# Gated linear attention and a mixture of experts on one core: the second chunk's experts by halves of the batch, transposes of its second half by DMA, and the decay's DMA on another queue

## The chip, the core and the metric

The kernel runs on one core of a Trainium2 chip. The metric is the device time of one execution in microseconds, the median over several executions.

A core has five engines that run side by side, each with its own queue of instructions, taken in order: PE (TensorE, matrix multiply into the banks of PSUM), ACT (ScalarE), DVE (VectorE), POOL (GpSimd) and SP (SyncE, which here only issues DMAs). ACT and POOL can issue DMAs too, and an engine does so in its own order of instructions.

## The reference

The first part is an attention with a gated state. Per batch and head it keeps a 48 x 48 state; each step of the sequence decays it by a sigmoid gate, adds an outer product of k and v, and reads it with q. The second part sends each of the 3072 tokens through four experts and sums their outputs by weights.

```python
# q, k, v, f_logit: (4, 8, 768, 48)
f = 1.0 / (1.0 + np.exp(-f_logit))
for t in range(S):
    state = f[:, :, t, :, None] * state + einsum('bhd,bhe->bhde', k[:, :, t], v[:, :, t])
    y[:, :, t] = einsum('bhd,bhde->bhe', q[:, :, t], state)
x = y.transpose(0, 2, 1, 3).reshape(3072, 384)
p = domain_probs / (domain_probs.sum(-1, keepdims=True) + 1e-09)
for e in range(4):
    h = np.maximum(x @ w1[e], 0.0)          # w1[e]: 384 x 1024
    out += p[:, e:e + 1] * (h @ w2[e])      # w2[e]: 1024 x 384
```

## The kernel before

**Chunks.** The sequence of 768 steps is cut into six chunks of 128 (`c` from 0 to 5), and each chunk is worked on for all four batches (`b`), eight heads at a time in four pairs. A chunk so gives 4 x 128 = 512 tokens. For each chunk the attention makes `xT`, the 512 tokens transposed to 384 features in three tiles of 128 partitions, and then the four experts (`e`) run on `xT`. The experts of one chunk and the attention of the next are interleaved.

**Attention of one chunk and batch.** ACT makes the gates (`gate1`, `gate2`, L256 and L260) from the loaded `f`. PE sums their logarithms along time with a triangular matrix (`pe_cs`, L264). ACT makes two tiles of exponentials of these sums (`exps`): `e[:, 0]` with the sign turned (L272 for the first chunk, L274 for the others) and `e[:, 1]` (L276). POOL or DVE multiplies q by the first and k by the second (`product`, L288). Q and K so made, tile `qk`, are needed with the features on the partitions, tile `QK`: in the first two chunks PE transposes them (`pe_tp`, L297, eight transposes a batch into PSUM) and ACT or DVE copies them out; in the others a DMA transposes them (`dma_tp`, L301, SP's queue). PE then multiplies K by Q (`pe_at`, L312), DVE masks the product (L316), and PE makes y from it, from v in bf16 (`vb`, L222 or L224) and from the state `sb` (`pe_y`, L323 and L327). y is copied out as `yb` and transposed to `xT`, in the first two chunks by PE (`pe_xt`, L352, three transposes a batch and a copy), in the others by DMA (`dma_xt`, L305).

**State.** PE multiplies k and v (`pe_kv`, L333), DVE adds that to the state `Sf` (L340), and POOL multiplies the sum by the chunk's total decay `egs` (L347) and casts it to `sb` (L348). The total decay is the last row of `e[:, 0]`, 192 numbers, which have to lie on partitions instead of along a row. In the first chunk it is made by small matmuls and an activation (L278). In the others two DMAs from SP's queue move it out of the tile of exponentials (`dma_egs`, L283).

**Experts.** A unit `h` is three matmuls into one PSUM bank (`mm_h`, L356), for 128 of the 1024 hidden features and either all 512 tokens or half of them (256). ACT (L364) or DVE (L362) evicts it with a relu to the tile `h`. A unit `o` is four matmuls of 384 columns (`mm_o`, L368); two units accumulate in one bank for one batch's 128 tokens, and ACT (L377) or DVE (L375, L379) scales the bank by the token's weight and adds it to `o`, which SP stores (L383). Four PSUM banks (`ps_m`) serve `h` and `o`; four more (`ps_t`) serve the attention, and two buffers hold the tile `h` of an expert. In the first chunk expert 0, and in the second chunk experts 0 and 1, run on half the tokens at a time: first on those of batches 0 and 1 (`LO`), then on those of batches 2 and 3 (`HI`), so that they can begin before the attention of the last batches is done. All other experts run on all 512.

**What sets the order.** Nothing in the program is scheduled by the compiler. Each step is an `Op` with a priority, the steps it needs, the buffers that it takes and frees, and an assumed cost on each engine that could do it. `Plan.run` goes through them in order of assumed time, gives each free engine the ready step of the best priority, and so fixes which engine does it and the order of each engine's queue. The steps are then emitted in that order, and semaphores keep them correct whatever their real durations are. `zip_units(hs, os)` gives `h` and `o` units alternating priorities, `unit[0]` counts them, and `attention(c, slot, gran)` puts the steps of a chunk's attention at slots counted from a unit (`base`).

**The head.** Before the first expert can run, its weights have to land. POOL issues their DMAs (L235) after the last q load of the first chunk has landed, and SP issues the loads (L228) one by one. Between the first attention steps PE runs matmuls on a constant tile (`busy`, L598) that nobody reads; the plan puts as many as fit in PE's planned idle time before the first expert:

```python
for o in done:
    if o.engine == "PE" and o.start <= first:
        o.pad, t = int((o.start - t) / 0.4), o.end
```

## Time and profile before

| | us |
|---|---|
| median of 11 runs | 304.79 (303.82 to 306.3) |
| the profiled execution, its own time | 304.19 |
| its span, first to last instruction | 302.5 |
| PE busy in the span | 291.7 |
| ACT, DVE, POOL busy | 170.4, 133.4, 98.3 |

The expert matmuls are most of it: L356 152.9 us in 648 matmuls (144 of them with 256 columns, 504 with 512) and L368 151.5 us in 776; spans of matmuls that follow each other overlap, so their sums are a little above the time they hold PE. In a line of a time line the first number is the start in us from the span's start, the second the length, then engine, line, operation, tiles, shape and count; brackets give the engine's idle time before it and what ended it. In a line of the waits stand the waiting line, what it waited for, the sum in us, the number of times and the longest.

### The profile page before, as it was taken

To read this page: it belongs to the slowest core of one execution; us is meant where nothing else is said; L and a number is where in the kernel's file an instruction comes from. 1 tells how busy PE (TensorE), PEld (TensorE's weight loads), DVE (VectorE), ACT (ScalarE), POOL (GpSimd) and SP (SyncE) were. 2 spreads that over 40 slices of the span, in tenths; PEclk is the share of its full clock that TensorE was granted. 3 is DMA by queue.
4 is the path that set the end of the run, shared out by engine and by line. 5 is a ranking of instruction groups with operands and counts; after the bars stand their busy time and mean duration, and the time that the engine had idled before them with its cause. 6 is when DMAs were issued, how large, how long until landed. Compare 5 with 4: busy or idle time off the path is not lost.

```text
span 302.5 us, 5499 instructions
## 1 busy us (share of the span) xinstructions
PE 291.7 (96%) x2120; PEld 167.9 (56%) x2120; DVE 133.4 (44%) x254; ACT 170.4 (56%) x305; POOL 98.3 (33%) x161
## 2 busy tenths in 40 slices
PE   6869999999999999999999999999999999999995
PEld 3548555556876566455555556555555555555553
DVE  6576003587755486506374425353315252201223
ACT  4765673757678363677455586435575444475440
POOL 4476501325666147342533442522342100000000
PEclk9598999999999999999999999999999999999999
DMA  9999999993999689989799978200322201100002
GB/s 151 194 188 203 208 208 201 187 138 108 149 188 134 95 132 171 242 118 173 122 193 164 201 157 154 48 15 24 104 61 49 51 13 42 70 8 2 0 0 104
DMA packets 135055, 36.08 MB, mean 119 GB/s; under 512 B 125405, under 2 KB 134237, under 8 KB 135029
## 3 DMA queue, kind: packets, MB, share of 16 engines
q1 hardware_dynamic: 128416, 29.40, 56.2%
q0 software_dynamic: 6576, 6.29, 12.8%
q8 instruction: 16, 0.26, 0.4%
q14 instruction: 11, 0.08, 0.1%
q10 hardware_dynamic: 36, 0.05, 0.1%
HBM read 31.51 MB, written 4.72 MB: 120 GB/s over the span
## 4 chain that ended last, share of the span: by engine, by line
PE 89%; DMA 4%; SPq 3%; DVE 1%; issue 1%; ACT 0%
PE ps_m L356 41%; PE ps_m L368 41%; SPq L228 3%; DMA w_sb<-in_moe_w_dram 2%; PE ps_t L312 2%; DMA q<-in_q_dram 2%; PE ps_t L327 1%; DVE qk L288 1%; PE ps_t L323 1%; PE ps_t L333 1%; PE ps_t L264 1%; PE ps_t L297 1%; PE ps_t L352 0%; ACT e L274 0%; DVE o L375 0%
## 5 line engine op out<-in xcount | busy, mean ns | idle before, releaser
L356 PE MATMUL ps_m<-xT,w_sb 128*128 128x512 bf16 (+1 forms) x648 | 152.9, 357 | 0.7 <-DMA w_sb<-in_moe_w_dram 0.7
L364 ACT ACTIVATE h<-ps_m 128x512 bf16<-128x512 f32 (+1 forms) x173 | 96.8, 562 | 100.7 <-PE ps_m L356 93.5
L368 PE MATMUL ps_m<-w_sb,h 128*128 128x384 bf16 (+1 forms) x776 | 151.5, 324 | 0.0
L368 PEld LDWEIGHTS <-h 128*128 128x128 bf16 x776 | 74.0, 98 | 58.3
L375 DVE SCALAR_TENSOR_TENSOR o<-ps_m,pn,o 128x384 f32<-128x384 f32 (+1 forms) x73 | 44.5, 611 | 105.8 <-PE ps_m L368 101.9
L356 PEld LDWEIGHTS <-w_sb 128*128 128x128 bf16 x648 | 62.2, 98 | 46.4 <-DMA w_sb<-in_moe_w_dram 0.8
L288 POOL TENSOR_TENSOR qk<-q,e 128x384 bf16<-128x384 f32 x19 | 22.7, 1195 | 47.7 <-ACT e L274 41.8
L362 DVE TENSOR_SCALAR h<-ps_m 128x512 bf16<-128x512 f32 (+1 forms) x43 | 23.7, 565 | 26.7 <-PE ps_m L356 23.8
L316 DVE TENSOR_TENSOR AT<-ps_t,mask 128x512 bf16<-128x512 f32 x48 | 30.2, 684 | 10.2 <-PE ps_t L312 10.2
L347 POOL TENSOR_TENSOR Sf<-Sf,egs 48x192 f32<-48x192 f32 x40 | 20.4, 509 | 41.0 <-DVE Sf L340 39.0
L288 POOL TENSOR_TENSOR qk<-k,e 128x384 bf16<-128x384 f32 x20 | 21.3, 1065 | 15.8 <-ACT e L276 10.5
L274 ACT ACTIVATE e<-ps_t 128x384 f32<-128x384 f32 x20 | 17.3, 865 | 3.9 <-POOL sb L348 2.1
L340 DVE TENSOR_TENSOR Sf<-Sf,ps_t 48x192 f32<-48x192 f32 x40 | 14.0, 350 | 6.2 <-PE ps_t L333 5.2
L235 POOL DMA_DIRECT2D w_sb<-in_moe_w_dram x11 | 9.0, 822 | 19.5 <-DMA k<-in_k_dram 16.3
L377 ACT ACTIVATE o<-ps_m,pn 128x384 f32<-128x384 f32 x22 | 12.8, 580 | 3.2 <-PE ps_m L368 2.3
L348 POOL CAST sb<-Sf 48x192 bf16<-48x192 f32 x40 | 13.6, 339 | 2.6
L224 POOL CAST vb<-v 128x384 bf16<-128x384 f32 x19 | 10.1, 554 | 9.4 <-DMA v<-in_v_dram 3.8
L256 ACT ACTIVATE ex<-f 128x768 f32<-128x768 f32 (+1 forms) x14 | 10.5, 747 | 4.2 <-DMA f<-in_f_logit_dram 4.2
L276 ACT ACTIVATE e<-ps_t 128x384 f32<-128x384 f32 x24 | 12.7, 530 | 0.0
L327 PE MATMUL ps_t<-vb,AT 128*128 128x48 bf16 x192 | 11.6, 186 | 0.2 <-ACT vb L222 0.2
L327 PEld LDWEIGHTS <-AT 128*128 128x128 bf16 x192 | 10.1, 98 | 2.3 <-issue 0.3
L260 ACT ACTIVATE gp<-ex 128x768 bf16<-128x768 f32 (+1 forms) x14 | 10.5, 749 | 0.3
(53 smaller groups left out, 130.3 us busy)
## 6 DMA issues: line engine op xcount, KB each, us to landing
out_dram<-o SPq DMA_DIRECT2D x23, 192.0 KB, 1.9
w_sb<-in_moe_w_dram POOLq DMA_DIRECT2D x5, 768.0 KB, 18.3
k<-in_k_dram SPq DMA_DIRECT2D x10, 384.0 KB, 5.8
q<-in_q_dram SPq DMA_DIRECT2D x10, 384.0 KB, 6.1
v<-in_v_dram SPq DMA_DIRECT2D x10, 384.0 KB, 5.4
f<-in_f_logit_dram SPq DMA_DIRECT2D x9, 384.0 KB, 4.8
w_sb<-in_moe_w_dram POOLq DMA_DIRECT2D x6, 384.0 KB, 9.0
f<-in_f_logit_dram SPq DMA_DIRECT2D x6, 192.0 KB, 4.5
```

The source lines that it names most:

```text
L274: nc.scalar.activation(out=e[:, 0].rearrange("t (d h) -> t h d", d=D), in_=cs[:, 0:HD].rearrange("t (i r d) -> t r i d", r=2, d=D), func=A ...
L288: engines[eng].tensor_tensor(out=tl("qk", c, b)[:, j, :, 0:D].rearrange("t (i r) d -> t i r d", r=2), in0=tl("qk"[j], c, b // 2)[:, hh(b), ...
L316: nc.vector.tensor_tensor(out=tl("AT", c, b)[:, r].rearrange("s i t -> s (i t)"), in0=tl("A", c, b, r).rearrange("s i t -> s (i t)"), in1= ...
L327: nc.tensor.matmul(out=y[:, h * D:(h + 1) * D], lhsT=AT[:, r, i, :], rhs=vb[:, h, :], start=(c == 0), stop=True, skip_group_check=True)
L340: nc.vector.tensor_tensor(out=Sf[rows, b], in0=Sf[rows, b], in1=KV[rows, :, r, :], op=ALU.add)
L347: nc.gpsimd.tensor_tensor(out=Sf[rows, b], in0=Sf[rows, b], in1=eg, op=ALU.mult)
L348: nc.gpsimd.tensor_copy(out=nb[rows, b, :, r * D:(r + 1) * D], in_=Sf[rows, b])
L356: nc.tensor.matmul(out=tl("hp", c, e, fc, n0)[:, n0:n1], lhsT=w1_sb[:, e, kk, fc * 128:(fc + 1) * 128], rhs=tl("xT", c)[:, kk, n0:n1], sta ...
L362: nc.vector.tensor_relu(out=dst, in_=src)
L364: nc.scalar.activation(out=dst, in_=src, func=AF.Relu)
L368: nc.tensor.matmul(out=tl("op", c, e, nt, part)[:, cols], lhsT=tl("h", c, e)[:, fc, nt * T:(nt + 1) * T], rhs=w2_sb[:, e, fc, cols], start ...
L375: nc.vector.scalar_tensor_tensor(out=o, in0=op, scalar=pe, in1=o, op0=ALU.mult, op1=ALU.add)
```

## The change

1. In the second chunk (`c == 1`) all four experts run first on the tokens of batches 0 and 1, then all four on those of batches 2 and 3, each expert in halves of 256 tokens. The tile `h` of such a half is a buffer of its own (`half_of`), still two buffers in all.
2. In the second chunk, batches 2 and 3 have Q, K and x transposed by DMA (as all later chunks do) and their K times Q products run as one group; batches 0 and 1 keep PE's transposes.
3. The total decay is moved by one DMA a batch, issued by ACT right behind the exponentials, in place of two issued by SP. For that the first tile of exponentials is laid out with 64 places a head of which 48 are used, the unused ones set to zero once at the start by POOL, so that the 128 partitions of `egs` are the row as it stands.
4. The slots of the attention move: of the third chunk by 10 units to the front, of later chunks by 6. The loads of the third chunk come 8 units later.
5. The number of matmuls on the constant tile in the head is made from other assumed lengths, and a load of the first chunk is assumed a little longer.

```diff
@@
+    for i in range(rooms["e"]):
+        pads["e", i] = const.tile([T, 2 * NP * P2 + HD], FP32, name=f"e{i}")
+        nc.gpsimd.memset(pads["e", i][:, 0:2 * NP * P2].rearrange("t (r d i) -> t r d i", r=2, i=NP)[:, :, D:P2, :], 0.0)
@@
+    def e_part(c, b, j):
+
+        e = tl("e", c, b)
+        if j == 0 and c > 0:
+            return e[:, 0:2 * NP * P2].rearrange("t (r d i) -> t i r d", r=2, i=NP)[:, :, :, 0:D]
+        e = e[:, 2 * NP * P2:] if j else e[:, 0:HD]
+        return e.rearrange("t (i r d) -> t i r d", d=D, r=2)
+
     def exps(c, b):
-        cs, e = tl("cs", c, b), tl("e", c, b)
+        cs = tl("cs", c, b)
+        src = cs[:, 0:HD].rearrange("t (i r d) -> t i r d", r=2, d=D)
+        for j in range(2):
+            o, i = e_part(c, b, j), src
+            if j == 0 and c > 0:
+                o, i = (x.rearrange("t i r d -> t r i d") for x in (o, i))
+            nc.scalar.activation(out=o, in_=i, func=AF.Exp, scale=1.0 if j else -1.0)
...
-        else:
-            nc.scalar.activation(out=e[:, 0].rearrange("t (d h) -> t h d", d=D),
-                                 in_=cs[:, 0:HD].rearrange("t (i r d) -> t r i d", r=2, d=D), func=AF.Exp, scale=-1.0)
-        nc.scalar.activation(out=e[:, 1], in_=cs[:, 0:HD], func=AF.Exp)
...
     def dma_egs(c, b):
-        last = tl("e", c, b)[T - 1:T, 0].rearrange("o (d r i) -> o r d i", r=2, d=D)
-        for r in range(2):
-            nc.sync.dma_start(out=tl("egs", c, b)[r * P2:r * P2 + D, :], in_=last[:, r])
+        nc.scalar.dma_start(out=tl("egs", c, b), in_=tl("e", c, b)[T - 1:T, 0:2 * NP * P2].rearrange("o (m i) -> o m i", i=NP))
@@
+    def half_of(c, n0):
+        return n0 // N2 if c == 1 else 0
+
     def relu(c, e, fc, n0, n1, eng):
-        dst, src = tl("h", c, e)[:, fc, n0:n1], tl("hp", c, e, fc, n0)[:, n0:n1]
+        dst, src = tl("h", c, e, half_of(c, n0))[:, fc, n0:n1], tl("hp", c, e, fc, n0)[:, n0:n1]
@@
-        op = P.add(f"ld {nm}{c}.{b}", {"DMA": cost or 1.05 * n}, lambda e: load(c, nm, b, n), prio,
+        op = P.add(f"ld {nm}{c}.{b}", {"DMA": cost or (1.05 if c else 1.1) * n}, lambda e: load(c, nm, b, n), prio,
@@
-            GS.append(P.add(f"egs {c}.{b}", {"DMA": 1.0}, on(dma_egs), s(3), deps=[ex], takes=[("egs", c, b)],
-                            frees=[("e", c, b)], lag=2.0) if c and more else None)
+            GS.append(P.add(f"egs {c}.{b}", {"ACT": 0.07}, on(dma_egs), s(0) + 0.15, deps=[ex], takes=[("egs", c, b)],
+                            frees=[("e", c, b)], lag=2.8) if c and more else None)
@@
-            if c < 2:
+            if (c, b) < (1, 2):
                 tq = P.add(f"tpq {c}.{b}", {"PE": 0.22}, on(pe_tp, 0), s(4), deps=[qm],
@@
-        pairs = [[b] for b in range(B)] if c < 2 else [[b, b + 1] for b in range(0, B, 2)]
+        pairs = [[b] for b in range(B)] if c == 0 else ([[0], [1]] if c == 1 else [[0, 1]]) + [[2, 3]]
@@
-            if c < 2:
+            if (c, b) < (1, 2):
                 xdone[c, b] = []
@@
     for c in range(C):
         u0 = unit[0]
+        if c + 1 < C:
+            base = u0 + {0: 10, 1: -10}.get(c, -6)
+            attention(c + 1, lambda b, s, base=base: base + 2 + 5 * b + s, 2)
+        if c + 2 < C:
+            for half in range(2):
+                for j, nm in enumerate("fkqv"):
+                    add_load(c + 2, nm, 2 * half, 2, u0 + {0: 38}.get(c, 30) + 4 * half + j, deps=wd[3, 1])
...
         elif c == 1:
             zip_units([], ol(0, E - 1, ALL))
-            for n0, n1, xs in ((0, N2, LO), (N2, NT, HI)):
-                zip_units(hl(c, 0, n0, n1, xs), [])
-                zip_units(hl(c, 1, n0, n1, xs), ol(c, 0, xs))
+            zip_units(hl(c, 0, 0, N2, LO), [])
+            for e in range(1, E):
+                zip_units(hl(c, e, 0, N2, LO), ol(c, e - 1, LO))
+            zip_units(hl(c, 0, N2, NT, HI), ol(c, E - 1, LO))
+            for e in range(1, E):
+                zip_units(hl(c, e, N2, NT, HI), ol(c, e - 1, HI))
+            zip_units(hl(c + 1, 0, 0, NT, ALL), ol(c, E - 1, HI))
+        elif c == 2:
+            pass
         else:
             zip_units(hl(c, 0, 0, NT, ALL), ol(c - 1, E - 1, ALL))
-        for e in range(2 if c == 1 else 1, E):
+        for e in range(E if c == 1 else 1, E):
             zip_units(hl(c, e, 0, NT, ALL), ol(c, e - 1, ALL))
-        if c + 1 < C:
-            base = u0 + (0 if c else 10)
-            attention(c + 1, lambda b, s, base=base: base + 2 + 5 * b + s, 2)
-        if c + 2 < C:
-            for half in range(2):
-                for j, nm in enumerate("fkqv"):
-                    add_load(c + 2, nm, 2 * half, 2, u0 + 30 + 4 * half + j, deps=wd[3, 1])
@@
-            o.pad, t = int((o.start - t) / 0.4), o.end
+            o.pad, t = int((o.start - t) / (0.42 if t < 7.0 else 0.25)), o.end
```

## The prediction

> **What bounds the kernel now.** I read the page first: engine shares, the 40 slices, the chain of work that ended last.
>
> ```profile
> PE 291.7 (96%) x2120; PEld 167.9 (56%) x2120; DVE 133.4 (44%) x254; ACT 170.4 (56%) x305; POOL 98.3 (33%) x161
> PE   6869999999999999999999999999999999999995
> PEclk9598999999999999999999999999999999999999
> ...
> PE 89%; DMA 4%; SPq 3%; DVE 1%; issue 1%; ACT 0%
> ```
>
> TensorE carries the run. From the fourth slice on its row is all nines, so a gain has to come from fewer PE instructions, from a PE wait, or from the head, where PE is not full and its clock row shows 5 and 8. Second came the waits of PE alone, which name all it waited for:
>
> ```profile
> PE ps_t L264 <- ACT gp L260: 1.9, 2, 1.1
> PE ps_m L598 <- DVE busy L143: 1.5, 1, 1.5
> PE ps_t L297 <- DVE qk L288: 1.4, 4, 0.5
> PE ps_t L352 <- ACT yb L222: 1.4, 1, 1.4
> PE ps_m L356 <- DMA w_sb<-in_moe_w_dram: 0.7, 1, 0.7
> ```
>
> All but the L297 row lie in the head. The time line of PE places three waits of that row at the second chunk, and the head's wait for weights at 22.92:
>
> ```profile
> 59.76 0.62 PE L297 MATMUL ps_t<-ident,qk 128*128 128x128 bf16 x8 [0.43 <-DVE qk L288]
> 61.34 0.62 PE L297 MATMUL ps_t<-ident,qk 128*128 128x128 bf16 x8 [0.31 <-DVE qk L288]
> 72.93 0.40 PE L297 MATMUL ps_t<-ident,qk 128*128 128x128 bf16 x4 [0.20 <-DVE qk L288]
> ...
> 22.92 1.46 PE L356 MATMUL ps_m<-xT,w_sb 128*128 128x256 bf16 x6 [0.67 <-DMA w_sb<-in_moe_w_dram]
> ```
>
> These 0.94 us are the only ones that an edit to the middle can win; after 73 us the sums by stretch show PE busy without a break. Third, I cut the head into stretches at the steps of the clock (start:end, length, busy time, instructions, granted clock, DMA share, GB/s):
>
> ```profile
> 4.54:7.95 3.41, 2.25 (x17) 1.00 1.32 191
> 7.95:11.37 3.42, 2.94 (x22) 0.50 1.27 194
> 11.37:14.78 3.41, 3.41 (x32) 0.50 1.34 197
> 14.78:18.19 3.41, 2.82 (x44) 1.00 1.41 189
> 18.19:21.61 3.42, 1.70 (x31) 1.00 1.26 182
> 21.61:25.02 3.41, 2.74 (x22) 0.50 1.23 203
> ```
>
> A stretch with 66% or 50% busy is followed by half clock, one with 83% is not. The drop at 21.61 falls on the first expert matmuls: nine of 256 columns take 2.10 us from 22.92 on the chain of waits, where six at full clock take 0.66 on that chain, so nine take about 1.0.
>
> [...] The trace does not decide if ACT and SP block each other: the one DMA on ACT's queue took 0.63 us beside SP's first loads. [...] the L288 product on DVE takes 1.34 us at 71.55 beside POOL's and 0.64 at 74.63 beside none.
>
> **The change part by part**, the order of each engine's instructions taken from the two programs.
>
> *PE work.* The third and fourth batch of the second chunk lose 16 transposes of Q and K and 6 of x. In the stream, eight L297 take 0.45 us (75.79 to 76.24) and three L352 0.17: 0.90 and 0.34 us less. Their QK products now come in one group of 16 (0.55 us at 103.27 before) in place of two of 8 (0.33 each): 0.11 less. All four experts of that chunk now run in halves: 48 matmuls of 512 columns become 96 of 256. On the chain three of 512 take 0.65 us and six of 256 take 0.66: the trace shows nothing to 0.01 per three, so at most 0.16 for 16 such groups; I take 0.12. Sum: 1.23 us less, on the path, since PE is full.
>
> *The PE wait at 72 to 75 us.* The 0.20 at 72.93 goes with its transposes. What comes next is worse. Nine units of 256 columns (27 matmuls, three a unit, 0.325 us a unit) now follow each other from 71.59, with nothing between them, on four PSUM banks. The fourth takes the bank of the last L368 group of the chunk before. Its reader L375 stands on DVE behind the first k product, which waits for ACT (71.51) and takes 1.33 beside POOL; so that reader starts at 72.80, as it did before, and ends at 73.40. The fourth unit would start at 71.59 + 3 x 0.325 = 72.57: a wait of 0.9. The relus then start on ACT at 73.0 (next part) and clear a bank each 0.37 us, DVE joins at about 74.5: no more than 0.1. Net +0.75 with the lost 0.20 (bounds 0.2 and 1.6).
>
> *Total decay from ACT's queue.* 32 issues leave SP, 16 come to ACT, most early ones in pairs behind four exponentials.
>
> ```profile
> L283 SPq DMA_DIRECT2D egs<-e x32: 507/582/2163, 63.3 to 187.9; - x32
> ```
>
> SP gains 32 x 0.58 = 18.6 us that no PE wait needed. On ACT, the first of a pair issues beside the exponentials; the second needs the third exponential and runs 0.58 beside the fourth (0.53), so relus behind it start some 0.45 us later. Four banks cover that except at 72.6, counted above: nothing more. If an issue also waits for SP's loads it is another matter (rival 2). Landing is 2 us, and the state on POOL needs it 8 us later.
>
> *Layout of the exponentials.* The L274 write has a stride of four floats in place of eight. It took 865 ns against L276's 530; it may fall to 530 or stay. I take 865; a gain would only shorten ACT, which is 56% busy. The three memsets on POOL (0.20 each by the row of U's memset) move the mask from 3.4 to about 4.1 us; its first reader runs at 11.36: nothing.
>
> *DMA transposes.* Two of Q and K land in 3.3 us, issued at about 74.1 and 75.4: 78.7, and PE wants them at 79.4 + 0.9. Two of x land some 10 us before their half is wanted, after four experts on the first half (about 21 us). Loads stand behind them on SP, the f of the third chunk by 0.4 us; its gate at 82.33 and the next L264 have about that much to spare. Later chunks start attention six units earlier: more room. I add 0.2 for these tight places (0 to 1.5).
>
> *The head.* The matmuls on the constant tile go from 20 to 35, all before the first expert. The start at 22.9 hangs on SP's loads and the weights, whose order is unchanged. Seven more lie before about 15 us and eight between 15 and 22.9. There PE idles 0.50 + 0.17 + 1.42 + 0.67 = 2.8 us and eight of 0.216 us at full clock are 1.7, so it still fits, by 1.1. The early seven cost 7 x 0.43 = 3.0 at half clock, which a rise at 11.37 instead of 14.78 pays back (3.41 us at full for half speed is 1.7 of full work, eight such matmuls). Stretches of 50% come to some 70 to 80% busy. [...] I hold it likelier than not that the clock stays: 2.10 - 1.05 = 1.05 us less. If not, 0; if the fillers delay the attention, up to +1.5.
>
> Sum: -1.23 + 0.75 + 0.2 - 1.05 = -1.3 us. The profiled execution took 304.19 (302.5 of span and 1.7 around it); the median of the runs is 304.79, 0.6 more, and I lay the difference on it: 303.5.
>
> **The rivals.**
> 1. *The fillers do not hold the clock* [...]. For: a longer filler waits for the same late v loads. Then -0.3: 304.5, no change that a measurement of this kernel can tell (0.3%, 0.9 us).
> 2. *ACT's issues wait for SP's loads.* At 56.88 SP spends 4.29 us on one load's issue, when the first pair comes (57.6). [...] ACT stands until 61.2 or beyond, the copies of Q and K (60.42 and 62.00) come 2 to 3 us late, and PE with them. Three further pairs meet loads of 1.2 to 2 us in halves, where four banks are 1.3 us of cover: some 0.5 each. -1.3 + 2.5 + 1.5 = +2.7: 307.5. It decides from an issue on ACT of about 1.2 us on. For: the longest on SP took 2.16. [...]
> 3. *More gain*: the half clock goes, the fourth unit does not wait, L274 is faster: -1.23 - 0.2 - 1.05 = -2.5: 302.3. Against: the wait follows from orders and durations that the trace shows.
>
> **How the numbers follow.** Forecast (302.8 to 303.9) 0.42, rival 1 (303.9 to 305.7) 0.20, rival 2 (over 305.7) 0.26, rival 3 (below 302.8) 0.12. Faster by over 0.3% is forecast and rival 3: 0.54. Rival 1 is mostly no change; with its slow edge to rival 2: 0.17 and 0.29. For eight in ten I leave out the lowest 0.03 and the upper part of rival 2: 302.0 to 306.8.
>
> **What would show it.** Right: 22 transposes fewer and a PE busy time down by what they cost; half clock no more around 22.9; a PE wait of about 0.9 us on an L356 renumbered for the new file, near 72.5, laid to the DVE reader of o; DMA issues on ACT's queue near 0.6 us. Wrong: such issues above 1.2 us and ACT idle behind them; PE waits on QK or xT for a DMA; a first expert matmul later than 23.5.

## The result and the profile after

The changed kernel took 302.85 us in the median (13 runs, 302.49 to 303.29), the kernel before, run beside it, 304.63 (48 runs, 303.23 to 306.3). The ratio is 0.9938, with a 95% interval of 0.9926 to 0.9951: faster by 0.6%. The profiled execution took 302.93 us, its span is 301.1. One run of experiment 4 (313.09 us, at a mean clock of 0.95) fell in a slow state and is left out of its figures. Lines of the program have moved: h is now L364 and its relus L375 (ACT) and L373 (DVE), o L379 and its DVE reader L386, the product L296, PE's transposes L305, K times Q L320, x transposed by DMA L313, the loads L232, the matmuls on the constant tile L614, the DMA of the decay L293.

The page of the kernel after, engine shares, the PE and clock rows, and the shares of the chain of work that ended last:

```profile
PE 290.0 (96%) x2161; PEld 170.5 (57%) x2161; DVE 129.1 (43%) x247; ACT 175.9 (58%) x324; POOL 98.5 (33%) x164
PE   6878999998999999999999999999999999999995
PEclk9999999999999999999999999999999999999999
PE 88%; SPq 4%; DMA 2%; issue 2%; DVE 1%; ACT 1%; ACTq 0%
```

The clock row is all nines: no half clock at the start, none at the first expert matmuls. PE's busy time fell by 1.7 us although it runs 41 more matmuls; part of that is half clock that is gone, since a matmul at half clock counts as busy for longer (one of 512 columns on the constant tile, alone in its row of the kernel before, takes 0.63 us at 12.44 at half clock and 0.38 at 17.62 at full). From the first o unit to the last 44 matmuls, where both kernels have full clock throughout, it fell from 259.9 to 258.9. The tenth slice, an 8 in PE's row, is the wait at 72.5 us. The first expert matmuls in the time line of PE before, and then, of the kernel after, all places of the head's end and the middle where PE stood:

```profile
22.92 2.10 PE L356 MATMUL ps_m<-xT,w_sb 128*128 128x256 bf16 x9 [0.67 <-DMA w_sb<-in_moe_w_dram]
```

```profile
21.88 1.16 PE L364 MATMUL ps_m<-xT,w_sb 128*128 128x256 bf16 x9 [0.33 <-ACT xT L226]
24.74 0.50 PE L364 MATMUL ps_m<-xT,w_sb 128*128 128x256 bf16 x3 [1.21 <-DVE psm L256]
58.76 0.62 PE L305 MATMUL ps_t<-ident,qk 128*128 128x128 bf16 x8 [0.36 <-DVE qk L296]
60.34 0.62 PE L305 MATMUL ps_t<-ident,qk 128*128 128x128 bf16 x8 [0.31 <-DVE qk L296]
72.53 2.12 PE L364 MATMUL ps_m<-xT,w_sb 128*128 128x256 bf16 x18 [0.81 <-DVE o L386]
86.85 0.81 PE L364 MATMUL ps_m<-xT,w_sb 128*128 128x256 bf16 x6 [0.31 <-ACT h L375]
```

The first nine expert matmuls take 1.16 us where they took 2.10, and PE reaches its first o unit at 31.30 where it did at 32.24. The wait of 0.81 at 72.53 is the one predicted. Two are new: 1.21 at 24.74 and 0.31 at 86.85. After 92 us PE is busy without a break, as before. The name in the bracket at 24.74 needs care. L256 is a reciprocal that reads no PSUM bank, and the last reader of that bank, L257, only begins at 24.74, so it cannot have freed anything then. The time line of weight loads (PEld) of the same kernel names another:

```profile
24.73 0.22 PEld L364 LDWEIGHTS <-w_sb 128*128 128x128 bf16 x3 [1.49 <-DMA w_sb<-in_moe_w_dram]
```

The unit there is the fifth in the plan and the first to use the second piece of the first expert's weights, and the weight load stands for that piece's DMA. Two experiments below test the two names.

### The profile page after: what moved, and what is told of

It reads as the page before. It is cut to its first block, busy times and chain, and to the rows that moved or that the text cites. A ratio compares the mean times of both kernels' runs of the same rounds, so it can differ in the third digit from the quotient of the medians.

```text
span 301.1 us, 5572 instructions
## 1 busy us (share of the span) xinstructions
PE 290.0 (96%) x2161; PEld 170.5 (57%) x2161; DVE 129.1 (43%) x247; ACT 175.9 (58%) x324; POOL 98.5 (33%) x164
## 4 chain that ended last, share of the span: by engine, by line
PE 88%; SPq 4%; DMA 2%; issue 2%; DVE 1%; ACT 1%; ACTq 0%
PE ps_m L364 41%; PE ps_m L379 40%; SPq L232 4%; DMA v<-in_v_dram 2%; PE ps_t L320 2%; PE ps_t L335 1%; PE ps_t L331 1%; PE ps_t L341 1%; PE ps_t L268 1%; DVE qk L296 1%; ACT e L288 1%; DVE o L386 0%; PE ps_t L360 0%; PE ps_m L614 0%; PE ps_t L305 0%
## 5 line engine op out<-in xcount | busy, mean ns | idle before, releaser
L375 ACT ACTIVATE h<-ps_m 128x512 bf16<-128x512 f32 (+1 forms) x192 | 101.7, 535 | 92.8 <-PE ps_m L364 89.1
L364 PE MATMUL ps_m<-xT,w_sb 128*128 128x512 bf16 (+1 forms) x696 | 152.6, 342 | 2.7 <-DVE psm L256 1.2
L379 PE MATMUL ps_m<-w_sb,h 128*128 128x384 bf16 (+1 forms) x776 | 152.0, 324 | 0.0
L379 PEld LDWEIGHTS <-h 128*128 128x128 bf16 x776 | 75.1, 98 | 58.8
L386 DVE SCALAR_TENSOR_TENSOR o<-ps_m,pn,o 128x384 f32<-128x384 f32 (+1 forms) x73 | 44.6, 612 | 117.1 <-PE ps_m L379 113.1
L364 PEld LDWEIGHTS <-w_sb 128*128 128x128 bf16 x696 | 65.5, 98 | 46.4 <-DMA w_sb<-in_moe_w_dram 1.9
L296 POOL TENSOR_TENSOR qk<-q,e 128x384 bf16<-128x384 f32 x19 | 22.9, 1211 | 32.8 <-ACT e L288 25.9
L373 DVE TENSOR_SCALAR h<-ps_m 128x256 bf16<-128x256 f32 (+1 forms) x40 | 20.4, 529 | 26.6 <-PE ps_m L364 24.9
L288 ACT ACTIVATE e<-ps_t 128x384 f32<-128x384 f32 x48 | 26.6, 667 | 6.1 <-PE ps_t L268 3.6
L296 POOL TENSOR_TENSOR qk<-k,e 128x384 bf16<-128x384 f32 x20 | 20.9, 1043 | 11.1 <-ACT e L288 6.2
L239 POOL DMA_DIRECT2D w_sb<-in_moe_w_dram x11 | 9.0, 825 | 21.9 <-DMA k<-in_k_dram 18.4
L388 ACT ACTIVATE o<-ps_m,pn 128x384 f32<-128x384 f32 x23 | 13.4, 581 | 2.4 <-PE ps_m L379 1.4
L614 PE MATMUL ps_m<-busy 128*128 128x512 bf16 x35 | 11.1, 423 | 1.5 <-DVE busy L144 1.5
```

Of the source, the lines that this page charges most:

```text
L288: nc.scalar.activation(out=o, in_=i, func=AF.Exp, scale=1.0 if j else -1.0)
L296: engines[eng].tensor_tensor(out=tl("qk", c, b)[:, j, :, 0:D].rearrange("t (i r) d -> t i r d", r=2), in0=tl("qk"[j], c, b // 2)[:, hh(b), ...
L364: nc.tensor.matmul(out=tl("hp", c, e, fc, n0)[:, n0:n1], lhsT=w1_sb[:, e, kk, fc * 128:(fc + 1) * 128], rhs=tl("xT", c)[:, kk, n0:n1], sta ...
L373: nc.vector.tensor_relu(out=dst, in_=src)
L375: nc.scalar.activation(out=dst, in_=src, func=AF.Relu)
L379: nc.tensor.matmul(out=tl("op", c, e, nt, part)[:, cols], lhsT=tl("h", c, e, half_of(c, nt * T))[:, fc, nt * T:(nt + 1) * T], rhs=w2_sb[:, ...
```

## The experiments

Theory 1: the gain is the head's clock (1.0 to 1.5 us) and PE's lost transposes (some 1.2), less the waits that came (0.8 at 72.5, 0.3 at 86.9). The rivals: theory 2, that all comes from the second chunk and the head's clock is beside the point; theory 3, that the queue of the total decay is what matters. Medians are compared with 302.85 for the changed kernel, and with the runs of the kernel before beside each (304.62 to 305.01).

**1. The old rule for the matmuls on the constant tile, in the changed kernel.**

```diff
-            o.pad, t = int((o.start - t) / (0.42 if t < 7.0 else 0.25)), o.end
+            o.pad, t = int((o.start - t) / 0.4), o.end
```

> The changed kernel with the number of matmuls on the constant tile worked out by the old rule again (30 lines of them in the program become fewer, spread as before). Theory 1, the head: about half of the gain is the full clock that the added matmuls hold, so the time goes up by 1.0 to 1.5 us from 302.85, to about 304.1; half clock shows again somewhere between 7 and 25 us, and the runs spread by 2 us or more where those of the changed kernel spread by 0.8. Theory 2, the second chunk: all of the gain is the lost transposes and the order of its experts, and the earlier start of the experts (21.9 in place of 22.9) is chance of the transfers: within 0.3 us of the changed kernel.

Measured: 304.20 us (20 runs, 303.0 to 306.06), ratio to the kernel before 0.9986 (0.9972 to 1.0). Its head in stretches (start:end, length, busy time, instructions, granted clock, DMA share, GB/s):

```profile
18.19:21.61 3.42, 1.78 (x26) 0.84 1.22 180
21.61:25.02 3.41, 2.88 (x28) 0.66 1.24 205
```

Half clock is back at the first expert matmuls (nine take 1.54 us in this execution), 1.35 us of the gain is gone, and the runs spread by 3.1 us, where the changed kernel's lie within 0.8. Theory 2 falls.

**2. The new rule alone, in the kernel before**, with the assumed length of a first load that goes with it.

```diff
-        op = P.add(f"ld {nm}{c}.{b}", {"DMA": cost or 1.05 * n}, lambda e: load(c, nm, b, n), prio,
+        op = P.add(f"ld {nm}{c}.{b}", {"DMA": cost or (1.05 if c else 1.1) * n}, lambda e: load(c, nm, b, n), prio,
...
-            o.pad, t = int((o.start - t) / 0.4), o.end
+            o.pad, t = int((o.start - t) / (0.42 if t < 7.0 else 0.25)), o.end
```

> The kernel before with only the new rule for the matmuls on the constant tile, and the assumed length of a first load that goes with it. Theory 1, the head: 1.0 to 1.5 us faster than before, about 303.4 against 304.63, the clock full throughout, the runs closer together, and a wait of about 1 us for the bank of the probabilities at 24 to 25 us that half clock had covered. Theory 2, the second chunk: within 0.3 us of the kernel before. A third way: the fillers delay the attention of the first chunk, and it is slower by 0.5 to 1.5 us.

Measured: 303.40 us (6 runs, 303.14 to 303.7), ratio 0.9957 (0.9942 to 0.9971): 1.3 us faster, the clock 1.00 throughout, the runs within 0.6. The wait came too, and in this kernel it is named after the weights in PE's own time line:

```profile
24.92 0.50 PE L356 MATMUL ps_m<-xT,w_sb 128*128 128x256 bf16 x3 [1.27 <-DMA w_sb<-in_moe_w_dram]
```

So the rule is worth 1.3 us with the rest of the change or without it. The kernel before says the same without an edit: of its 49 runs beside this one, the two with a mean clock of 0.998 took 303.32 and 303.57 us, the 22 at 0.994 took 304.57 in the mean, the 12 at 0.989 took 305.23. (A mean does not tell where the fall lies, and not every fall costs as much: the profiled execution has 0.981 and took 304.19.)

The rule makes the full clock likely, not certain. In all 13 runs of the changed kernel the mean clock is 1.00, but with the same rule it is 0.993 or 0.994 in 3 of the 21 runs of experiment 4, 1 of 10 of experiment 8 and 2 of 6 of experiment 12; the three of experiment 4 took 305.1 to 305.3 us, some 1.3 more than the others.

**3. The decay's DMA on SP, at ACT's place in the emitted order.**

```diff
-        nc.scalar.dma_start(out=tl("egs", c, b), in_=tl("e", c, b)[T - 1:T, 0:2 * NP * P2].rearrange("o (m i) -> o m i", i=NP))
+        nc.sync.dma_start(out=tl("egs", c, b), in_=tl("e", c, b)[T - 1:T, 0:2 * NP * P2].rearrange("o (m i) -> o m i", i=NP))
```

> The changed kernel with the one DMA of the total decay issued by SP in place of ACT, at the same place of the emitted order; every other instruction is unchanged. Theory 1: the queue is worth nothing to the end: within 0.3 us of 302.85, but the issues on SP that meet its loads take 1 to 4 us and the wait of 0.31 us at 86.85, behind ACT's third exponential and issue, shrinks. Theory 3, the queue matters: SP's issues stand behind the loads that it issues, the states on POOL come late, and PE waits for sb: 0.5 to 2 us slower.

Measured: 305.04 us (14 runs), ratio 1.0 (0.9987 to 1.0013): the whole gain is gone. SP's semaphore waits for this line and its issues (duration in ns, least/median/most, first and last start in us):

```profile
L293 SPq EVENT_SEMAPHORE  x16: 17/17/5759, 50.9 to 180.8; - x16
L293 SPq DMA_DIRECT2D egs<-e x16: 470/544/3142, 56.7 to 180.9; - x16
```

The longest that SP stood for exponentials which ACT had not yet made is 5.76 us, at 50.9, with loads queued behind it. That stand reached no PE wait: PE's wait for the DVE reader of o comes at 72.68, 0.15 later than in the changed kernel, which is what the head had already lost. PE's time line shows where time was lost:

```profile
93.58 0.49 PE L364 MATMUL ps_m<-xT,w_sb 128*128 128x256 bf16 x3 [1.23 <-ACT h L375]
...
166.03 3.40 PE L364 MATMUL ps_m<-xT,w_sb 128*128 128x512 bf16 x15 [1.39 <-DMA xT<-yb]
```

The first is a late f load: ACT waits 1.6 us for it with relus behind. In SP's order two issues of the decay, 1.18 us together, stand ahead of it (first two lines), and it is issued 1.27 us later than in the changed kernel (last line):

```profile
86.10 1.18 SPq L293 DMA_DIRECT2D egs<-e  x2
...
88.64 0.57 SPq L232 DMA_DIRECT2D f<-in_f_logit_dram  x1
```

```profile
87.37 0.57 SPq L232 DMA_DIRECT2D f<-in_f_logit_dram  x1
```

Before the second, too, an issue of the decay stands between two transposes of x. So it was SP's time in its order that was short. The wait of 0.31 us at 86.85 is gone here: in the changed kernel ACT's issue, which ends at 86.37, held the relu of 86.41. Theory 3 has the right sign, but not its way (no PE wait for sb) nor its size (0.5 to 2 us). This run mixes the queue with the place; the fifth was meant to take them apart.

**4. PE transposes for the second chunk's third and fourth batch again.**

```diff
-            if (c, b) < (1, 2):
+            if c < 2:
...
-        pairs = [[b] for b in range(B)] if c == 0 else ([[0], [1]] if c == 1 else [[0, 1]]) + [[2, 3]]
+        pairs = [[b] for b in range(B)] if c < 2 else [[0, 1], [2, 3]]
```

> The changed kernel with Q, K and x of the second chunk's third and fourth batch transposed by PE again and their products in two groups (22 transposes more, 6 evictions more for ACT or DVE); the experts' order by halves stays. Theory 1: PE is full there, so the time goes up by the transposes' 0.90 + 0.34 and the groups' 0.11, less what falls into the 0.81 us wait at 72.5: 0.6 to 1.35, about 303.9. Rival: the transposes all fall into waits (0.81 at 72.5), or the DMA transposes cost as much by late relus: within 0.3 us.

Measured: 303.96 us (21 runs, 303.67 to 305.31), ratio 0.998 (0.9968 to 0.9992): 1.1 us slower than the changed kernel. In the traces, PE reaches its last 44 matmuls 0.93 us later (292.91 against 291.98), of which 0.19 already stands at the end of the head; the 1.35 us of transposes and groups are met by waits that are gone (0.81 at 72.5 is 0.27, and the 0.31 at 86.85 is not there). That would leave 0.50; of the 0.74 behind the head, 0.24 were not placed. Transposes by DMA pay in PE's time, not one for one.

**5. The decay's DMA on SP (as in experiment 3), planned where the kernel before had it.**

```diff
-            GS.append(P.add(f"egs {c}.{b}", {"ACT": 0.07}, on(dma_egs), s(0) + 0.15, deps=[ex], takes=[("egs", c, b)],
-                            frees=[("e", c, b)], lag=2.8) if c and more else None)
+            GS.append(P.add(f"egs {c}.{b}", {"DMA": 1.0}, on(dma_egs), s(3), deps=[ex], takes=[("egs", c, b)],
+                            frees=[("e", c, b)], lag=2.0) if c and more else None)
```

> The changed kernel with the one DMA of the total decay issued by SP and planned where the kernel before had it (four slots after the exponentials, on the DMA queue, 1.0 us of assumed length); the run before it moved only the queue and left the issue right behind the exponentials, where SP stood up to 5.8 us for ACT with loads behind it. Theory 1 (it was the place on SP, not the queue, that cost 2.2 us): within 0.4 us of 302.85. Theory 3 (SP has no room for these issues in the changed kernel, since transposes of the second chunk have come to its queue): 1 to 2.5 us slower, with PE waits on xT or on ACT behind f, as in the run before.

Measured: 309.71 us (6 runs, 308.29 to 311.65), ratio 1.0162 (1.0127 to 1.0197): 6.9 us slower than the changed kernel, more than at ACT's place. The third chunk's xT comes late. PE's time line, and the stretch from the second wait on (columns as in experiment 1):

```profile
100.33 0.40 PE L320 MATMUL ps_t<-QK 48*128 48x128 bf16 x8 [0.58 <-DMA QK<-qk]
...
125.90 7.67 PE L364 MATMUL ps_m<-xT,w_sb 128*128 128x512 bf16 x27 [3.50 <-DMA xT<-yb]
```

```profile
125.80:129.20 3.40, 3.30 (x9) 0.54 1.30 216
```

The clock adds to it: 0.54 over the 3.4 us behind that wait, and in this execution also a fall at the first expert matmuls (nine take 1.50 us) in spite of the new rule, so that 1.4 us of the loss stands before the second chunk's first transposes (60.18 against 58.76). The two runs with the highest mean clock, 0.994, took 308.3 and 308.8; by their clock they seem to be without that fall.

Theory 1, that only the place cost, falls with this issue at this place, but 6.9 is far above theory 3's 1 to 2.5 too, and SP's queue does not show it: SP stands idle from 119.79 until the first of these transposes of x goes out at 120.67. It is y that is late. With the assumed length of the decay on SP the plan puts the third chunk's attention later in PE's own order: its last K times Q group starts at 116.33, where it was 109.91, and the last y at 120.71, where it was 114.29; the waits and the half clock before that place account for some 1.9 of these 6.4 us. So this run, too, does not take the queue and the place apart: the place in SP's order came with another plan for all engines. That the queue matters rests on experiment 3.

**6. Both products of the second chunk's late batches on POOL**, so that DVE reads the last o bank at once.

```diff
-            pe = {"DVE": 0.47} if c == 0 and b == B - 1 else {"DVE": 0.47, "POOL": 1.36} if c == 0 else {"DVE": 0.6, "POOL": 1.0} if c == 1 else {"POOL": 1.0}
+            pe = {"DVE": 0.47} if c == 0 and b == B - 1 else {"DVE": 0.47, "POOL": 1.36} if c == 0 else {"DVE": 0.6, "POOL": 1.0} if c == 1 and b < 2 else {"POOL": 1.0}
```

> The changed kernel with the products of Q and K for the second chunk's third and fourth batch kept from DVE (POOL alone makes them), so that DVE reads the last o bank at once. Theory 1: the PE wait of 0.81 us at 72.5 goes, and nothing takes its place: 302.85 - 0.7 = 302.1, or a little more where POOL's four products of 1.2 us end at about 75.5 and the second DMA transpose then lands 0.5 us before PE wants it. Rival: the wait comes back as one for QK or for a bank that ACT's relus clear: within 0.3 us.

Measured: 307.45 us (6 runs), ratio 1.0089 (1.0066 to 1.0113), a miss for both expectations. The wait at 72.5 shrank to 0.23 as meant, and the kernel lost 4.6 us: a change of the costs that the plan assumes moves the whole plan behind it. PE's time line, and SP's, in which q of a later chunk now stands between the two transposes of x:

```profile
123.37 7.54 PE L364 MATMUL ps_m<-xT,w_sb 128*128 128x512 bf16 x27 [2.79 <-issue]
```

```profile
116.71 1.83 SPq L313 DMA_TRANSPOSE xT<-yb  x1
118.97 0.37 SPq L232 DMA_DIRECT2D q<-in_q_dram  x1
119.46 1.93 SPq L313 DMA_TRANSPOSE xT<-yb  x1
```

The second of these lands at 119.5 + 3.8 = 123.3, when PE goes on. In the changed kernel it is issued at 116.1 and lands 2.3 us later, at 118.4, and PE wants it at 120.05: 1.6 us of room, which no wait of the profile shows. The issue is 3.4 us later here; most of that is y, which the new plan puts 2.9 us later on PE (its last part starts at 117.16, not 114.29), and the load of q has a small part in it. The stretches of this kernel before and behind its wait (columns as in experiment 1) show what the wait cost besides:

```profile
120.00:123.40 3.40, 0.52 (x3) 0.96 0.93 168
123.40:126.80 3.40, 3.40 (x9) 0.54 1.59 249
```

PE all but idle for 3.4 us, then half clock for about as long: 3.40 x 0.46 = 1.6 us of work lost. With 2.79 for the wait, 0.26 for one at 120.09, 0.13 more at 86.8 and 0.58 less at 72.5, that makes 4.2 of the 4.4 us between the two spans.

**7. The weights of the tokens (psm, pn) made earlier**, a test of the name in the bracket at 24.74.

```diff
-    pdone = P.add("probs", {"DVE": 0.9}, lambda e: probs(), 4, deps=[pp] + xdone[0, B - 1], frees=[("ps_m", "pp")])
+    pdone = P.add("probs", {"DVE": 0.9}, lambda e: probs(), 4, deps=[pp] + xdone[0, 1], frees=[("ps_m", "pp")])
```

> The changed kernel with the weights of the tokens (the instructions on psm and pn) placed into DVE's idle time ahead of the last copy of y in the head. The waits of PE name DVE's reciprocal for the 1.21 us at 24.74; the row of weight loads names the DMA of the expert weights for the same time. If DVE's probabilities held the bank: 0.8 to 1.2 us faster, near 301.8. Theory 1 (the second piece of expert weights lands at 24.7, and the fifth unit, the first to use it, stands there): within 0.3 us of 302.85, the wait still at 24.7 to 24.9.

Measured: 302.89 us (6 runs, 302.69 to 303.32), the changed kernel's time. PE waits 1.19 us at 24.70, now named after the weights' DMA. The name in the bracket of the changed kernel was wrong.

**8. The second piece of weights assumed later**, so that work which doesn't need it goes first.

```diff
-        op = P.add(f"w {i}", {"DMA": 2.25 if i < 6 else 4.5}, lambda _: None, -400 if i == w_last else -460 + i, deps=[iss], lag=1.5)
+        op = P.add(f"w {i}", {"DMA": 2.25 if i < 6 else 4.5}, lambda _: None, -400 if i == w_last else -460 + i, deps=[iss], lag=2.7 if i == 1 else 1.5)
```

> The changed kernel with the second piece of expert weights assumed to land 1.2 us later, so that the plan puts the products of the state and four units on the third and fourth batch ahead of the first unit that needs this piece; the number of matmuls on the constant tile stays. Theory 1 (the wait of 1.21 us at 24.74 is for that piece): 0.8 to 1.2 us faster, near 301.9, no wait for weights after the first unit. Rival (a bank held by DVE): a wait of the same size remains near 24, on the fifth unit: within 0.3 us.

Measured: 303.22 us (10 runs, 302.92 to 304.16), ratio 0.9948 (0.9932 to 0.9964): no gain, a miss for theory 1. The wait for the second piece is gone, but two lines of PE's time line tell the rest:

```profile
22.80 1.16 PE L364 MATMUL ps_m<-xT,w_sb 128*128 128x256 bf16 x9 [0.88 <-DMA w_sb<-in_moe_w_dram]
...
28.61 3.08 PE L364 MATMUL ps_m<-xT,w_sb 128*128 128x256 bf16 x18 [0.34 <-DVE h L373]
```

In this execution the first piece landed at 22.8, not at 21.9, and a wait for DVE's relu came instead. The runs together explain it. In those with full clock in the head PE reaches its first o unit at nearly one time, 31.3 to 31.5, whatever the first expert unit did:

| kernel | first expert unit | wait for the second piece | first o unit |
|---|---|---|---|
| before (half clock) | 22.92 | none | 32.24 |
| 1, old rule (half clock) | 23.09 | none | 31.93 |
| changed kernel | 21.88 | 1.21 | 31.30 |
| 2, new rule alone | 22.00 | 1.27 | 31.48 |
| 3, decay on SP | 22.91 | 0.32 | 31.44 |
| 6, products on POOL | 22.82 | 0.32 | 31.35 |
| 8, second piece late | 22.80 | none | 31.53 |

Experiments 4, 7, 11 and 12 fit in, with 31.27 to 31.49. So 0.9 of the 1.21 us is only the early start of that execution; the unit that needs the second piece starts at 24.7 to 24.9 in all of these that wait for it. With that wait removed, the wait of 0.34 for a relu on DVE came, and PE was no earlier.

**9. The decay on ACT's queue alone, in the kernel before** (with the padded tile of exponentials that it needs, as in the change; nothing else of it).

```diff
-        for r in range(2):
-            nc.sync.dma_start(out=tl("egs", c, b)[r * P2:r * P2 + D, :], in_=last[:, r])
+        nc.scalar.dma_start(out=tl("egs", c, b), in_=tl("e", c, b)[T - 1:T, 0:2 * NP * P2].rearrange("o (m i) -> o m i", i=NP))
...
-            GS.append(P.add(f"egs {c}.{b}", {"DMA": 1.0}, on(dma_egs), s(3), deps=[ex], takes=[("egs", c, b)],
-                            frees=[("e", c, b)], lag=2.0) if c and more else None)
+            GS.append(P.add(f"egs {c}.{b}", {"ACT": 0.07}, on(dma_egs), s(0) + 0.15, deps=[ex], takes=[("egs", c, b)],
+                            frees=[("e", c, b)], lag=2.8) if c and more else None)
```

> The kernel before with the total decay alone changed as in the change: one DMA a batch from ACT's queue right behind the exponentials, the padded tile of exponentials that this needs; order of the experts, transposes, slots and constant-tile matmuls as before. Prediction's step (the queue is worth nothing where no PE wait needs SP): within 0.4 us of the kernel before, no new PE wait over 0.3 us. Theory 3, revised after the run with the issues at their old place on SP (+6.9 us in the changed kernel): the queue is worth something only where SP also has the second chunk's transposes, so nothing here either. Rival: SP is the tight queue already before, and it is 1 us or more faster; or ACT's issues in front of relus make it 0.5 us or more slower.

Measured: 305.52 us (22 runs, 304.16 to 306.7), ratio 1.0024 (1.001 to 1.0039): 0.9 us slower, neither the nothing of the prediction nor a gain, but the 0.5 or more of the last expectation. Part of it is the clock, which falls more often in these runs (the mean clock is 0.989 or lower in 13 of the 22, against 13 of the 27 of the kernel before beside them): at equal mean clock it is 0.6 to 0.7 slower (at 0.994 a mean of 305.03 against 304.35, at 0.989 305.87 against 305.28). Of the 1.3 us between the two profiled executions 0.5 stand at the end of the head, where half clock falls in both, and 0.4 between 72 and 90 us, where PE is busy for 17.43 us and not for 17.80; the rest was not placed. Alone this part loses; what of ACT's order makes it lose is not shown.

**10. The DMA transposes alone, in the kernel before**, in the old order of experts.

```diff
-            if c < 2:
+            if (c, b) < (1, 2):
...
-        pairs = [[b] for b in range(B)] if c < 2 else [[b, b + 1] for b in range(0, B, 2)]
+        pairs = [[b] for b in range(B)] if c == 0 else ([[0], [1]] if c == 1 else [[0, 1]]) + [[2, 3]]
```

> The kernel before with only the transposes of the second chunk's third and fourth batch given to DMA (22 PE transposes fewer), in the old order of its experts, where two experts and not four run on the first half before the second half is wanted. If DMA transposes pay by themselves: 1 us faster, as PE's work falls by 1.1 us. Theory 1 (the four experts on the first half are the cover for the DMA's way): PE waits for xT of the second half by DMA, several us in one place near 95 us, and others for QK; 5 to 17 us slower (the upper end is what the plan itself leaves idle on PE).

Measured: 318.82 us (4 runs), ratio 1.0462 (1.043 to 1.0495): 14.2 us slower. PE's time line:

```profile
93.92 0.80 PE L264 MATMUL ps_t<-gp,Ub 128*128 128x384 bf16 x2 [4.89 <-ACT gp L260]
99.10 4.60 PE L356 MATMUL ps_m<-xT,w_sb 128*128 128x256 bf16 x27 [4.38 <-DMA xT<-yb]
```

PE is busy 11.9 of the 24 us from 76 to 100. With two experts on the first half, PE has run out of expert work by 83 us, before the second half has come through the DMAs, and then waits for one step of the attention after another: the 4.89 is for gates of the third chunk, whose f load ACT waits for until 92.15. The four experts by halves give PE work for that time. But this run keeps the old slots and the decay on SP as well, so it shows that the edit cannot stand alone, not which of the three it lacks most.

**11. One pair exchanged on DVE in the changed kernel**: after the plan has run, the reader of the last o bank goes ahead of the product of k. `defer` moves a step, and what needs it, behind another step in the list that is emitted.

```diff
     done = P.run()
+    defer("k 1.2", "ev_o 0.3.3.0")
```

> The changed kernel with one pair on DVE exchanged: its reader of the last o bank of the first chunk goes ahead of the product of k for the third batch, and nothing else of any engine's order differs. (The run that took both products from DVE removed most of this wait, 0.81 to 0.23, but its whole plan moved, and the third chunk's xT came 2.8 us late.) Theory 1: the wait at 72.5 falls from 0.81 to 0.2 or less, QK of the third batch lands 0.6 later, which has about 2 us of room, and the time falls by 0.5 to 0.8: 302.2. Rival: the time is given back at the next wait (86.85, or the third chunk's xT by DMA near 120): within 0.3 us of 302.85.

Measured: 302.54 us (6 runs, 302.42 to 303.02), ratio 0.9924 (0.9909 to 0.9939). The place in PE's time line:

```profile
72.46 2.00 PE L364 MATMUL ps_m<-xT,w_sb 128*128 128x256 bf16 x15 [0.23 <-ACT h L375]
```

The wait fell from 0.81 to 0.23, and PE's last 44 matmuls start 0.36 us earlier (291.62), although this execution came 0.15 later out of the head: 0.5 us kept to the end, the lower end of what theory 1 said. The median moved by 0.3; against the changed kernel, run in another group, that is less than the intervals can part.

**12. The same, and the Q and K transposes of the first two batches one expert unit later.**

```diff
+    defer("k 1.2", "ev_o 0.3.3.0")
+    defer("tpk 1.0", "h 0.3.6.0")
+    defer("tpq 1.0", "h 0.3.6.0")
+    defer("at 1.1", "o 0.2.3.1")
+    defer("at 1.0", "h 0.3.7.0")
+    defer("tpk 1.1", "h 0.3.7.0")
+    defer("tpq 1.1", "h 0.3.7.0")
```

> The run before it (the reader of o ahead of the product) and, on PE, the transposes of Q and K of the second chunk's first two batches each one expert unit later, with the K times Q groups behind them, so that the waits of 0.36 and 0.31 us for DVE's products at 58.8 and 60.3 are filled. Theory 1: 0.2 to 0.5 us more off, about 301.8; part of it comes back as waits of 0.2 each for the copies of QK and for the masked products. Rival: all of it comes back there: the same as the run before it.

Measured: 301.95 us (6 runs, 301.4 to 303.31), ratio 0.9907 (0.9887 to 0.9928), the fastest of all. The waits at 58.8 and 60.3 are gone, none has come in their place, and the last 44 matmuls start at 290.81, 0.8 before those of experiment 11. It beats the kernel before by 0.9%; that it beats the changed kernel rests on the traces and on 0.9 us between medians of different groups, whose intervals just touch.

## Why the prediction was right, and where it was not

**The sum.** It said -1.3 us for the profiled execution: that went from 304.19 to 302.93, -1.26. By place: PE reaches its first o unit 0.94 us earlier (the head, predicted 1.05). From there to its last 44 matmuls it takes 260.68 us in place of 260.86, with 1.04 less work (predicted 1.23) and 0.86 more waiting (predicted 0.75, and 0.2 for tight places). That makes 1.12. The other 0.3 of the 1.4 us between the spans lie behind the last matmuls, where SP waits 0.8 us for stores to land and not 1.1; no term covers that, and that the totals agree to 0.04 is in part luck.

The median went by -1.78, and the forecast of 303.5 was 0.65 too high: 302.85 lies at the lower edge of what the prediction called its forecast (302.8 to 303.9). The term that was mis-sized is the last one, where the prediction added 0.6 for the distance of the profiled execution to the median. That distance was the kernel before's own: half clock falls differently from one run to the next (its runs spread by 3.1 us; see the clocks under experiment 2). A kernel that keeps full clock lost the distance along with the half clock: its profiled execution and its median agree to 0.1. The head's gain should have been worked out against the median run, not the profiled one: about 1.05 and the 0.4 from 304.19 to 304.63; experiments 1 and 2 give 1.35 and 1.3.

**PE work (-1.23).** 22 transposes fewer, as said, and 1.04 us less work from the first o unit on. The halves cost a little more than the 0.12 taken: the 48 matmuls of 512 columns that went took 13.1 us in all (132.9 less 119.8), the 96 of 256 that came 13.4 (32.9 less the 19.5 of experiment 2, whose clock is full), sums in which ends overlap. Experiment 4 is 0.74 us slower behind the head, near what the term less the waits that PE's transposes cover would be.

**The PE wait at 72 to 75 us (+0.9, net +0.75).** 0.81 at 72.53, behind the DVE reader that was named. Working the order of one engine's queue against the banks was enough to see it; experiment 11 shows the cause by exchanging that one pair. Not foreseen was the smaller one at 86.85: third-chunk exponentials and the issue behind them ahead of a relu, 0.31 us; the step on ACT's queue had weighed this kind of delay and put it at nothing. One reading ahead of the steps was off: the product of 0.64 us at 74.63 in the kernel before was not beside an idle POOL, whose own product ran to 74.86. One that was, at 15.71, took 0.55. But so did three in the head beside a product of POOL's, at 6.32, 10.08 and 13.29 (0.55 to 0.56 us), so POOL's company alone does not make the 1.33 at 71.55; what does was not tried.

**The decay on ACT's queue (nothing).** On the issues themselves it was right. In the changed kernel they take (columns as in experiment 3)

```profile
L293 ACTq DMA_DIRECT2D egs<-e x16: 477/478/537, 56.6 to 177.7; - x16
```

and at 57.6, while one load's issue held SP for 4.19 us, an issue on ACT took no longer (0.48 us). Rival 2, an estimate that no trace had shown, falls. But the step said that SP gains 18.6 us that no PE wait needed, and so priced the move at nothing. Experiments 3 and 9 show otherwise: alone the move costs 0.9 us, and with the rest of the change the same issues on SP, behind the exponentials, cost 2.2. SP's time, which no PE wait of the kernel before needed, was needed in the changed kernel. Which other part of the change needs it, the transposes or the earlier slots, was not tested. The total came out because the sum took the changed kernel as a whole, where ACT issues them and they cost nothing but the 0.31 us above.

**Layout of the exponentials, DMA transposes.** The write with the padded stride takes up to 881 ns where it took 865 in the mean: it stayed. No PE wait on QK or xT for a DMA came in the changed kernel, as said. The 0.2 for tight places was put to the second chunk; the tight place that the runs found is the third chunk's xT, with 1.6 us of room. The order by halves and the new slots and loads (points 1 and 4 of the change) were not run apart from the rest, so what they are worth by themselves is open.

**The head (-1.05).** The clock stayed full, experiments 1 and 2 measured what that is worth, and rival 1 falls. The way to it was not the one worked out. The stretch from 18.19 was to come from 50% to some 70 to 80% busy; it came to 58% (last section), with three matmuls on the constant tile where there had been two, and the clock stayed full all the same. That the clock would stay was an estimate, and the prediction's own lines gave no bound to reach: it set 66% and 50%, followed by half clock, against 83%, but its stretch 7.95:11.37 is busy for 2.94 of 3.42 us, 86%, and half clock follows it. So the gain of the head was right in its size, and that the clock held was in part luck. Two more things were off without touching the result: the first expert unit did not stay at 22.9 in every execution, and the second piece of weights, hidden by half clock before, became the wait that ends the head. That is why an earlier first unit brought nothing.

## What to carry to other kernels

Work out each part of a change against the kernel it will stand in, not the one it leaves: here the queue's move is a loss alone and worth 2.2 us beside the rest. Look at the room of transfers that nobody waits for, since another engine for a few products moved the plan and turned 1.6 us of room into a wait of 2.8 and half clock behind it; and where an edit changes what a plan assumes, compare the orders of all engines before laying the loss to the edit. Where a clock falls differently from run to run, measure the gain of holding it on medians, and look at their spread as well (here 3.1 us before and 0.8 after); and where a wait's named releaser could not have freed the buffer, read the weight loads' row before acting on it.

## What the hardware showed that was not expected

**When the clock falls.** The kernel before was at half clock after a stretch with PE busy 66% of the time, and after one with 86%. The changed kernel in two stretches of the head (start:end, length, busy time, instructions, clock, DMA share, GB/s):

```profile
18.19:21.61 3.42, 1.97 (x34) 1.00 1.03 156
21.61:25.02 3.41, 1.93 (x18) 1.00 1.22 192
```

58% and 57% busy, and the clock after them is full. Both stretches lie where those of the kernel before do, since this clock shows no step to lay them by. Busy shares of such stretches do not sort the cases in these traces: 50, 66 and 86% were followed by half clock, 57, 58 and 83% were not. So no threshold follows.

**Two long waits were paid twice.** In the middle of the run, where PE is otherwise full, the waits of 2.8 us (experiment 6) and 3.5 us (experiment 5) were each followed by a clock of 0.54 over the next 3.4 us, some 1.6 us more; the wait of 1.39 us in experiment 3 was not (1.00 behind it). No length between these was tried.

**When the first weights land.** With the new rule the first expert unit began at 21.9 to 22.0 in some executions (the changed kernel, experiments 2, 4, 7 and 11) and at 22.8 to 23.0 in others (3, 5, 6, 8 and 12), with nothing between among the runs profiled. PE's last transposes of y ahead of it are 0.4 to 0.7 us later in the second group as well, so it is not the weights alone. What decides wasn't tried; the table under experiment 8 shows that it doesn't reach the first o unit.
